# Where the first of two maxima pieces stands inside an output product

## The chip, the cores and the metric

The kernel runs on one core of one Trainium2 chip. The metric is the device time of one execution in microseconds; the median of three timed runs counts. One further execution was profiled, and all views of the profile come from it.

## The reference

Two multi-head attentions over 2048 positions, each with 32 heads of 18 columns, stand side by side in the output. A looks at 8 positions, two apart; B at all of them.

```python
def _A_ref(x, wqkv, wo):                    # B, S, D = 1, 2048, 576; H = 32; Dh = 18
    ...
    logits = jnp.einsum("bhsd,bhswd->bhsw", q, kg) * scale    # 8 neighbours, dilation 2
    ...
    o = jnp.einsum("bhsw,bhswd->bhsd", attn, vg)
    return (lambda x, *d: x.transpose(*d))(o, 0, 2, 1, 3).reshape(B, S, D) @ wo

def _B_ref(x, wqkv, wo):
    ...
    scores = jnp.einsum("bhqd,bhkd->bhqk", q, k) * scale
    p = _softmax(scores, axis=-1)
    o = jnp.einsum("bhqk,bhkd->bhqd", p, v)
    return (lambda x, *d: x.transpose(*d))(o, 0, 2, 1, 3).reshape(B, S, D) @ wo

a = _A_ref(A_x, A_wqkv, A_wo)
b = _B_ref(B_x, B_wqkv, B_wo)
return jnp.concatenate([a, b], axis=-1)
```

## The kernel before

The schedule is written out by hand: each engine runs its instructions in the order in which the Python code issues them, and a wait holds up all that stands behind it on that engine. After the projections (until about 500 us) come 512 steps of B. A step is one group of four heads, one block of 512 queries and one tile of 128 keys. In it TensorE computes four scores of 128 keys by 512 queries (`score`, line 229), one for each head; ScalarE takes their exponentials (line 235); and TensorE weighs the values with the exponentials of the step before (`weigh`, line 700, eight matmuls over all 128 rows of the array).

A score uses 56 rows of the array, and so the array is worked as two halves of 64 rows: heads 0 and 2 run on half 0, heads 1 and 3 on half 1.

The exponentials need the greatest score of each query beforehand. TensorE therefore also computes *maxima pieces*, 128 queries by 512 keys (`take`, line 159), and VectorE reduces each one to its maximum (`reduce`, line 166). A step normally holds three pieces. Each stands behind a score and runs on the other half (`maximum(1 - r)`).

Everything on TensorE ends in one of PSUM's eight banks. One (`po`) belongs to the weighing. Four form the ring "scores", three the ring "else"; `bank(kind)` gives the next of a ring, and the first matmul into it waits until the bank's last content has been read. Pieces use the ring "else", so that each one waits for the reduction of the piece (or the reading of the sum) that had its bank.

A's attention itself is computed by GpSimd beside all this, in eight runs of 256 positions, with a few small operations on VectorE and ScalarE (lines 850, 859, 866). Its output product (`sums_of_a`) is done in 32 parts, 128 positions by 288 columns, for which 27 matmuls of 288 columns are needed; B's output products (`sum_of`) have the same shape with 30. Both call `beside`, which deals the matmuls out to the two halves: 14 on half 0 and 13 on half 1 for A, 15 and 15 for B. Each half has a sum of its own, in a bank of "scores" and one of "else". `beside` issues them by turns, half 0, half 1, half 0 and so on (line 1001). ScalarE (line 918) and VectorE (line 919) add A's two sums; for B VectorE does both (lines 1020 and 1021).

A product stands inside a step, ahead of head 2 or head 3:

```python
if inside and h == (3 if 3 in places else 2):
    inside.pop(0)()
es.append(score(g, b, kt, h, h in places, ...))
```

As long as there are maxima to compute, `beside` puts two further pieces inside the product, one into each half's list. These are the "first" and the "second" piece. After the product a bank of "else" is passed over (`rings["else"].append(...)`), because it still holds a sum; the step's remaining piece, "the next piece" below, then takes the bank of the first one. Where the product stands ahead of head 2, head 2's score (half 0), the next piece (half 1) and head 3's score (half 1) come behind it; where it stands ahead of head 3, head 3's score (half 1) and the next piece (half 0).

Of the kernel before, what the change touches and what calls it, by code (L numbers as in the profile page):

```python
# [59 lines left out]
def two_attentions(ctx: ExitStack, tc, xa, wa, woa, xb, wb, wob, out):  # L60
# [19 lines left out]
    def bank(kind=None):  # L80
        r = rings[kind or ring]
        r.append(r.pop(0))
        return p_bank.tile([128, 512], F32, name=f"bank{r[-1]}")
# [124 lines left out]
    def maximum(r):  # L208

        n, i = divmod(given[r], PIECES)  # L210
        given[r] += 1
        if n not in blocks:
            blocks[n] = block(*divmod(n, NB))
        take, reduce = blocks[n]
        piece = (r, i // 2 // NB, i // 2 % NB, i % 2)
        ps = take(*piece)
        return lambda: reduce(ps, *piece)
# [121 lines left out]
    with (tc.tile_pool(name="x", bufs=1, side="right") as xp,  # L339
# [104 lines left out]
        if True:  # L444
# [238 lines left out]
            turns = len(work_list) - NT + 4  # L683
# [122 lines left out]
    def local(j):  # L806
# [103 lines left out]
        def sums_of_a(h):  # L910
            his, los = zip(*wo["a"])
            w = his[:4], los[:4], his[4], los[4]
            cols = slice(288 * h, 288 * h + 288)
            if h == 0:
                st["y"] = ys["a", j, st["n"]] = work.tile([128, D], F32, name="y", bufs=4)
            one, two = beside("scores", *(halves(r, 0, w, st["x"], cols, slice(0, 128), True) for r in range(2)))
            y = st["y"][:, cols]
            nc.scalar.activation(y, two, AF.Copy)
            behind_scores.append(lambda: nc.vector.tensor_add(y, one, y))
# [67 lines left out]
    def beside(kind, *both):  # L987

        sums_ = [bank(k)[:, :288] for k in (kind, None)]
        turns = [[(sums_[r], *ab, i == 0, i == len(t) - 1) for i, ab in enumerate(t)] for r, t in enumerate(both)]  # L990
        pair = kind and sum(given) + 2 <= NG * NB * PIECES * 2
        if pair:

            for r in range(2):
                turns[r].insert(4 + 6 * r, None)
        for i in range(max(map(len, turns))):
            for r in range(2):
                if i < len(turns[r]):
                    if turns[r][i]:
                        ps, a, b, start, stop = turns[r][i]  # L1000
                        nc.tensor.matmul(ps, a, b, start=start, stop=stop)  # L1001
                    else:
                        maximum(r)()
        if pair:

            rings["else"].append(rings["else"].pop(0))
        return sums_

    def sum_of(y, t, h, chunks, kind=None):

        pos, cols = slice(128 * t, 128 * t + 128), slice(288 * h, 288 * h + 288)
        both = []
        for r in range(2):
            both.append([])
            for c, (hi, lo) in enumerate(chunks):
                at = slice(64 * r, min(64 * r + 64, hi.shape[0]))
                whi, wlo = wo["b"][c]
                both[r] += [(a[at, pos], w[at, cols]) for a, w in ((hi, whi), (hi, wlo), (lo, whi))]
        one, two = beside(kind, *both)
        nc.vector.tensor_copy(y, one)  # L1020
        nc.vector.tensor_add(y, two, y)
# [149 lines left out]
```

## Time and profile before

| | |
|---|---|
| timed runs | 1653.38, 1653.39, 1655.6 us; median 1653.39 us |
| the profiled execution's own time | 1650.43 us |
| its span, first to last instruction | 1648.7 us, mean granted TensorE clock 0.999 |
| busy: TensorE, VectorE, ScalarE, GpSimd | 1639.2, 1400.6, 1223.6, 960.5 us |
| 2048 maxima reductions (L166) on VectorE | 1291.3 us, 684 ns each |
| 2048 exponentials (L235) on ScalarE | 1060.1 us, 611 ns each |

In the views, PE is TensorE's matmuls, PEld its weight loads, DVE VectorE, ACT ScalarE, POOL GpSimd, SP the engine that issues most transfers. L159 is line 159 of the kernel. A row of the timeline gives start, duration, engine, line, operation, output and inputs, shapes and a count, and in brackets how long the engine had been idle and what ended that. Matmuls are pipelined, so their durations overlap: the distance between two starts on one half is what a matmul costs there.

### The profile page before, as it was taken

What the parts mean: (1) busy time and instruction counts of PE and PEld (TensorE: products, weight loads), DVE (VectorE), ACT (ScalarE), POOL (GpSimd) and SP (SyncE); (2) the same over time, 40 slices, a digit from 0 to 9 for tenths busy, and PEclk for the clock granted to TensorE, in tenths of its full rate; (3) what the DMA queues carried; (4) which work ended last, traced back from release to release, by engine and by line L of the source; (5) the groups of instructions that cost most, each with busy time, mean ns of one, the idle gap of its engine ahead of it and who ended that gap; (6) DMA issues with size and microseconds to landing.
All of it is one profiled execution on the core that took longest, in us unless ns stands there. A gap on an engine that the chain in (4) does not pass through costs nothing.

```text
span 1648.7 us, 33732 instructions
## 1 busy us (share of the span) xinstructions
PE 1639.2 (99%) x12906; PEld 935.6 (57%) x12906; DVE 1400.6 (85%) x2386; ACT 1223.6 (74%) x2419; POOL 960.5 (58%) x800
## 2 busy tenths in 40 slices
PE   9999999999999999999999999999999999999999
PEld 7999788999433344344344344344344344344676
DVE  5199899999899989989889889889889989888533
ACT  6414432111899998998998998998998998998544
POOL 2306642210185995994994995994994997920000
PEclk9999999999999999999999999999999999999999
DMA  8937955522515346156238225617526132034201
GB/s 250 238 114 205 255 165 139 133 87 90 95 51 97 99 132 123 68 130 137 67 91 159 83 70 154 131 50 130 125 79 126 58 105 78 21 114 140 83 37 58
DMA packets 188353, 188.22 MB, mean 114 GB/s; under 512 B 118384, under 2 KB 132208, under 8 KB 186464
## 3 DMA queue, kind: packets, MB, share of 16 engines
q1 hardware_dynamic: 183328, 174.53, 40.2%
q0 software_dynamic: 4032, 10.63, 3.2%
q8 instruction: 101, 1.65, 0.4%
q10 hardware_dynamic: 832, 0.92, 0.2%
q14 instruction: 60, 0.49, 0.1%
HBM read 113.16 MB, written 88.12 MB: 122 GB/s over the span
## 4 chain that ended last, share of the span: by engine, by line
PE 96%; DMA 1%; DVE 1%; ACT 1%; issue 1%; POOL 0%; SPq 0%; POOLq 0%; ACTq 0%
PE po L700 30%; PE bank L229 26%; PE bank L322 15%; PE bank L159 13%; PE bank L1001 7%; PE bank L259 5%; DVE mx L166 1%; DMA dqk<-olo 0%; POOL xlo L370 0%; PE bank L976 0%; DMA dqk<-ohi 0%; DMA first<-xb 0%; ACT xhi L369 0%; SPq L363 0%; ACT olo L461 0%
## 5 line engine op out<-in xcount | busy, mean ns | idle before, releaser
L166 DVE TENSOR_REDUCE mx<-bank 128x1 f32<-128x512 f32 x2048 | 1291.3, 684 | 146.0 <-PE bank L159 108.5
L235 ACT ACTIVATE e<-bank 128x512 f32<-128x512 f32 x2048 | 1060.1, 611 | 91.2 <-PE bank L229 54.5
L159 PE MATMUL bank<-ks,qs 54*128 54x512 f32 x2048 | 751.4, 423 | 1.5 <-DVE mx L166 0.5
L229 PEld LDWEIGHTS bank<-qs,ks 56*128 56x128 f32 x2048 | 328.7, 185 | 449.5 <-ACT e L235 424.6
L229 PE MATMUL bank<-qs,ks 56*128 56x512 f32 x2048 | 579.4, 425 | 0.0
L700 PE MATMUL po<-e,v 128*19 128x512 f32 x4096 | 539.6, 599 | 0.0
L159 PEld LDWEIGHTS bank<-ks,qs 54*128 54x128 f32 x2048 | 341.8, 185 | 19.8 <-DVE mx L166 11.9
L832 POOL TENSOR_TENSOR pr<-aq,akv 128x1024 f32<-128x1024 f32 x72 | 158.4, 2200 | 27.2 <-DMA akv<-dpart 24.6
L700 PEld LDWEIGHTS po<-e,v 128*19 128x19 f32 x4096 | 69.5, 97 | 180.0 <-issue 169.5
L875 POOL TENSOR_TENSOR pr<-lg,akv 128x1024 f32<-128x1024 f32 x72 | 158.2, 2197 | 0.6
L836 POOL TENSOR_TENSOR pr<-pr 128x1024 f32<-128x1024 f32 x64 | 152.5, 2383 | 5.0
L651 ACT ACTIVATE ohi<-bank 128x512 f32<-128x512 f32 (+1 forms) x56 | 30.5, 595 | 147.6 <-issue 109.6
L322 PE MATMUL bank<-xhi,ahi 64*128 64x512 f32 (+1 forms) x448 | 114.1, 387 | 0.0
L322 PE MATMUL bank<-xhi,alo 64*128 64x512 f32 (+1 forms) x448 | 111.4, 387 | 0.0
L322 PE MATMUL bank<-xlo,ahi 64*128 64x512 f32 (+1 forms) x448 | 109.3, 388 | 0.2
L876 POOL TENSOR_TENSOR pr<-pr 128x512 f32<-128x512 f32 x72 | 92.2, 1281 | 5.6
L370 POOL TENSOR_TENSOR alo<-raw,ahi 128x512 fp32r<-128x512 f32 (+1 forms) x14 | 17.6, 1254 | 120.5 <-ACT ahi L369 105.8
L463 POOL TENSOR_TENSOR olo<-olo,ohi 128x512 fp32r<-128x512 f32 x36 | 46.1, 1294 | 66.2 <-ACT ohi L462 64.2
L1001 PE MATMUL bank<-wohi,at 64*128 64x288 f32 x512 | 68.5, 301 | 0.0
L322 PEld LDWEIGHTS bank<-xhi,ahi 64*128 64x128 f32 (+1 forms) x448 | 64.8, 181 | 3.5
L322 PEld LDWEIGHTS bank<-xhi,alo 64*128 64x128 f32 (+1 forms) x448 | 62.5, 182 | 3.5
L736 POOL TENSOR_TENSOR o<-o,rec 128x512 f32<-128x512 f32 x29 | 37.3, 1287 | 45.6 <-ACT e L235 24.7
(196 smaller groups left out, 1769.7 us busy)
## 6 DMA issues: line engine op xcount, KB each, us to landing
do<-n SPq DMA_DIRECT2D x28, 512.0 KB
da<-ohi SPq DMA_DIRECT2D x52, 256.0 KB
dpart<-da SPq DMA_DIRECT2D x16, 702.0 KB
akv<-dpart SPq DMA_DIRECT2D x16, 702.0 KB
out<-y SPq DMA_DIRECT2D x32, 288.0 KB
qs<-dqk SPq DMA_DIRECT2D x30, 288.0 KB
ks<-dqk SPq DMA_DIRECT2D x30, 288.0 KB
at<-dao SPq DMA_DIRECT2D x64, 128.0 KB
```

What stands on the lines that cost most here:

```text
L159: nc.tensor.matmul(ps, qs[at, b, p, 128 * t : 128 * t + 128], ks[at, p, 512 * k : 512 * k + 512], start=True, stop=True)
L166: nc.vector.tensor_reduce(mx[:, r, p, t, k : k + 1], ps, axis=AX.X, op=ALU.max)
L229: nc.tensor.matmul(ps, ks[at, p, 128 * kt : 128 * kt + 128], qs[at, b, p], start=True, stop=True)
L235: nc.scalar.activation(e, ps, AF.Exp, scale=SCALE)
L259: nc.tensor.matmul(ps, a, b, start=c == i == 0, stop=c == 4 and i == 1)
L322: nc.tensor.matmul(ps, a, b, start=start, stop=stop)
L700: nc.tensor.matmul(po[32 * i : 32 * i + 19], vs[g][:, kt, 19 * i : 19 * i + 19], es[i], start=kt == 0, stop=kt == NT - 1)
L832: nc.gpsimd.tensor_mul(pr, ap(st["q"][:, 2 * c], (SUB, 2), (0, W), (1, SUB)), window(st["k"], c))
L836: nc.gpsimd.tensor_add(st["pr"], st["pr"], pr)
L875: nc.gpsimd.tensor_mul(at, ap(st["lg"], (0, 2), (SUB, W), (1, SUB)), window(st["v"], c))
L876: nc.gpsimd.tensor_add(at[:, :, :4], at[:, :, :4], at[:, :, 4:])
L1001: nc.tensor.matmul(ps, a, b, start=start, stop=stop)
```

## The change

In `beside`, each half's list of matmuls gets a placeholder for its piece. Half 0's (`r = 0`) stood at place 4 and now stands at place 6; half 1's (`r = 1`) stays at place 10.

```diff
         if pair:
 
             for r in range(2):
-                turns[r].insert(4 + 6 * r, None)
+                turns[r].insert(6 + 4 * r, None)
```

So the first piece is issued behind six pairs of product matmuls instead of four, and four places ahead of the second piece instead of six. This concerns the 34 products with pieces in them: all 32 of A and two of B. Nothing is added or removed.

## The prediction

> **What bounds the kernel now.** I read the page first: engine shares, granted clock, the chain that ended last.
>
> ```profile
> PE 1639.2 (99%) x12906; PEld 935.6 (57%) x12906; DVE 1400.6 (85%) x2386; ACT 1223.6 (74%) x2419; POOL 960.5 (58%) x800
> PEclk9999999999999999999999999999999999999999
> PE 96%; DMA 1%; DVE 1%; ACT 1%; issue 1%; POOL 0%; SPq 0%; POOLq 0%; ACTq 0%
> ```
>
> TensorE (PE) is on 96% of the chain, at full clock throughout. A microsecond saved or lost on it is one of the span, unless another engine is late there. But "busy" counts modelled ends and hides short waits inside the stream. So next: the waits of weight loads (PEld), and VectorE's groups between 600 and 1520 us, which count the products that the change touches.
>
> ```profile
> PEld bank L159 <- DVE mx L166: 11.9, 41, 0.5
> L919 DVE TENSOR_TENSOR y<-bank,y 128x288 f32<-128x288 f32 x32 | 14.3, 448 | 0.0
> ```
>
> 41 times the load for a maxima piece (L159) waited for a maximum reduction (L166) on VectorE to free its PSUM bank, 11.9 us in all. The 32 rows of L919 are the sliding attention's output products; with two of the full attention's, in the last scheduled steps, 34 products hold two pieces each. In the two programs' instruction order just these 34 first pieces move on TensorE; the order on the other queues stays. Then I read the timeline of each of the 34. Here is one, TensorE's rows first, then its load, VectorE and ScalarE (ACT). Columns: start us, us, engine, line, what, count, idle before.
>
> ```profile
> 610.24 0.43 PE L1001 MATMUL bank<-wohi,at 64*128 64x288 f32 x4
> 610.51 0.29 PE L1001 MATMUL bank<-wolo,at 64*128 64x288 f32 x2
> 610.64 0.29 PE L1001 MATMUL bank<-wohi,at 64*128 64x288 f32 x2
> 610.99 0.49 PE L159 MATMUL bank<-ks,qs 54*128 54x512 f32 x1
> 610.99 0.40 PE L1001 MATMUL bank<-wohi,at 64*128 64x288 f32 x1
> 611.23 0.29 PE L1001 MATMUL bank<-wolo,at 64*128 64x288 f32 x1
> 611.32 0.33 PE L1001 MATMUL bank<-wohi,at 64*128 64x288 f32 x2
> 611.89 0.39 PE L159 MATMUL bank<-ks,qs 54*128 54x512 f32 x1
> 612.52 0.40 PE L159 MATMUL bank<-ks,qs 54*128 54x512 f32 x1
> 612.63 0.51 PE L229 MATMUL bank<-qs,ks 56*128 56x512 f32 x2
> 613.08 1.05 PE L700 MATMUL po<-e,v 128*19 128x512 f32 x8
> 610.98 0.18 PEld L159 LDWEIGHTS bank<-ks,qs 54*128 54x128 f32 x1 [0.28 <-DVE mx L166]
> 610.24 0.69 DVE L166 TENSOR_REDUCE mx<-bank 128x1 f32<-128x512 f32 x1 [0.22 <-PE bank L159]
> 610.85 0.68 DVE L166 TENSOR_REDUCE mx<-bank 128x1 f32<-128x512 f32 x1
> 611.51 0.69 DVE L166 TENSOR_REDUCE mx<-bank 128x1 f32<-128x512 f32 x1
> 612.34 0.69 DVE L166 TENSOR_REDUCE mx<-bank 128x1 f32<-128x512 f32 x1
> 612.73 0.41 ACT L918 ACTIVATE y<-bank 128x288 f32<-128x288 f32 x1 [1.44 <-PE bank L1001]
> ```
>
> L1001 x2 is a pair, one matmul on each half of the array. Pairs follow every 0.13 us (610.51, 610.64), so the first piece was due on half 0 at 610.77. Its bank was held by the reduction of 610.24, which ends at 610.93; the load starts 0.05 later, at 610.98, and nothing covers it: the piece shows 0.49 us, not 0.39, so I let it stream from 611.09. That is 0.32 us after it was due. Half 1's next product, behind it in the queue, waits too.
>
> **Part by part.** Nothing is added or removed; the first piece goes behind two more pairs. The second stands where it was.
>
> *Early products.* In 17 of the 34 the product stands ahead of head 2. The load of 610.98 is their first; the sixteenth:
>
> ```profile
> 1486.80 0.18 PEld L159 LDWEIGHTS bank<-ks,qs 54*128 54x128 f32 x1 [0.28 <-DVE mx L166]
> ```
>
> (The 17th, at 1533.5, waits alike.) Two more pairs take 2 x 0.13 = 0.27 us, unrounded, of the 0.32: the piece is due at 611.04 and, its bank being free when it was, still streams at 611.09, but with two pairs behind it instead of ahead. Gain so far 0.27.
>
> Then two banks come due sooner than before. The second piece takes the bank of the reduction at 610.85, free at 611.53: load 611.58, stream 611.68. Half 1 reaches it after four products (4 x 0.13) from 611.09, at 611.62, where it began at 611.89. Waits 0.06; gain 0.21. Third, the piece after the product, also on half 1, takes the first piece's own bank. That reduction starts at 611.51, as before, and ends at 612.20: load 612.25, stream 612.35. Half 1 gets there after a piece and three products. A piece holds its half 0.24 us, as a pair of rows of another product shows, of which more below:
>
> ```profile
> 634.65 0.42 PE L1001 MATMUL bank<-wohi,at 64*128 64x288 f32 x3
> 634.78 0.40 PE L159 MATMUL bank<-ks,qs 54*128 54x512 f32 x1
> 635.02 0.32 PE L1001 MATMUL bank<-wohi,at 64*128 64x288 f32 x2
> ```
>
> So it is due at 611.68 + 0.24 + 3 x 0.13 = 612.32, waits some 0.03, and streams at 612.35 against 612.52. Gain 0.165, my value (0.16 to 0.17 with unrounded starts). Queued behind this new wait are head 3's score (L229) on half 1 and the eight weighings (L700) at 613.08, which need both halves; they come 0.165 earlier. ScalarE waits for those scores, had been idle 1.44 us, and stays ahead. VectorE does two reductions 0.61 apart (610.24, 610.85); the second piece's comes at about 612.13 instead of 612.34, which it can serve. 17 x 0.165 = 2.8 us.
>
> The bounds of this term: 0 if the two new waits take all, 0.27 if they take none.
>
> *Late products.* In the other 17 the product stands ahead of head 3, and half 0 ends last. A typical one, then the one that waits longest:
>
> ```profile
> 640.98 0.52 PE L1001 MATMUL bank<-wohi,at 64*128 64x288 f32 x2
> 641.12 0.47 PE L159 MATMUL bank<-ks,qs 54*128 54x512 f32 x1
> 642.77 0.39 PE L159 MATMUL bank<-ks,qs 54*128 54x512 f32 x1
> 643.08 0.62 PE L700 MATMUL po<-e,v 128*19 128x512 f32 x3
> 641.63 0.69 DVE L166 TENSOR_REDUCE mx<-bank 128x1 f32<-128x512 f32 x1
> 888.56 0.18 PEld L159 LDWEIGHTS bank<-ks,qs 54*128 54x128 f32 x1 [0.18 <-DVE mx L166]
> ```
>
> Here half 0 still had head 2's score to finish, so its fourth product came at 640.98. The piece was due at 641.11 and streams from 641.20 (0.47 is 0.08 over 0.39): it lost 0.08, half 1 more, but half 1 has time left. Two places later it streams unhindered at 641.38; its reduction moves from 641.63 to 641.81 and ends at 642.50, so the next piece could stream at 642.65; it is due at 642.77 - 0.08 = 642.69. Gain 0.08, margin 0.04. Twelve like this gain 0.06 to 0.08: 12 x 0.07 = 0.85 us. Two with a later release (this load and one at 1386) lose about 0.2, and the shift covers it: 0.4. Three (634.78 above is one) come late for another reason and find their bank free: the piece shows 0.40 and follows its pair by 0.13. They gain nothing and lose nothing; their margin for the next piece is some 0.01 to 0.04.
>
> *Sum:* 2.8 + 0.85 + 0.4 = 4.05, say 4.0 us. The profiled execution took 1650.43 (span 1648.7 and 1.7 around it): it would be 1646.4. The median of the three timed runs is 1653.39, 3.0 above it; I take the gain off that: **1649.4 us**.
>
> *What a realignment may cost.* Steps after the first product run earlier against DMAs and GpSimd (POOL). The trace has two accidents of that kind, a transfer that VectorE met before it landed and a small tensor operation that took 1.33 us beside a GpSimd one:
>
> ```profile
> 907.97 0.25 DVE L733 RECIPROCAL den<-den 128x16 f32<-128x16 f32 x1 [1.25 <-DMA den<-o]
> 1376.27 1.33 DVE L850 TENSOR_TENSOR am<-am 128x64 f32<-128x64 f32 x1
> ```
>
> Each costs about 1 us. One may go or one may come: 0 taken, from -2 to +2.
>
> **Rivals.** *More gain.* If matmuls of the two halves had to start in program order, each 512-wide piece would hold up both; half 1 would then reach the second piece at about 611.72 and the next at 612.49, both after their banks are free, and the early products would keep the whole 0.27: 17 x 0.267 + 1.25 = 5.8 us, 1647.6. Against it: after the first piece the program has two wohi products, half 1's and half 0's, before the first wolo, yet the rows show one wohi at 610.99, the wolo at 611.23, and the other wohi at 611.32. So the halves pass each other. By the Trainium skill, "TensorE: Matmul & The Clock Gate", section "The mechanism", matmuls start and end strictly in program order even on different row groups; these rows differ from it, and by that rule it would be this rival. 12%.
>
> *Part of the gain.* The next piece's wait costs 0.10 more than I reckon, as the load exposed at 610.98 did: early products gain 0.065, 17 x 0.065 + 1.25 = 2.3 us, 1651.1. An accident more does the same. For it: the margins of 0.03 to 0.06 are at the edge of what the rows resolve. With the low end of my forecast, 26% within 0.2%.
>
> *Slower.* The next piece is tied to the first piece's bank. If that first piece were not waiting for the reduction of 610.24 but for something that moves along with it, such as a restart of TensorE, it would come 0.27 + 0.10 later than now: its reduction at 611.88, the next piece's stream at 612.72 instead of 612.52; in a late product at 642.84 instead of 642.77. 17 x 0.20 + 17 x 0.07 = 4.6 us, 1658.0. It decides from a reduction 0.17 late in the early products. Against it: the load follows the reduction's end by 0.05 us in every early product, and where the bank was free there was no wait. 9%.
>
> **How the numbers follow.** The bound of 0.2%, 3.3 us, is about what a measurement of this kernel can tell from no change. Forecast as worked out, gain over 3.3: 53%. With the 12% of more gain, faster 65%; same 26%; slower 9%. The range takes in the greater gain with an accident gone (5.8 + 1 = 6.8 us, 1646.6) and, at the other end, the partial gain with two accidents more (1653.1) and 0.9 us for the scatter of the timed runs, which lie 2.2 us apart (1653.38 to 1655.6): 1654.0. Slower by 4.6 is left out.
>
> **What would show it.** Early products: the first piece's load waits about 0.03 instead of 0.28 behind six pairs; the piece after the product starts about 2.11 us after the product's first row instead of 2.28, its load just behind the first piece's reduction; the L700 some 2.67 us after the product instead of 2.84. The row L159 <- L166 falls from 11.9 by about 4. Late products: L700 0.07 nearer. I am wrong if the first piece still waits as long, if its reduction in the early products comes later than 1.3 us after the product's start, or if the piece after it gives the 0.27 back.

## The result, and the profile after

The changed kernel is faster: 1649.07 us in the median of six runs (1645.07 to 1650.25) against 1655.57 of six runs of the kernel before (1653.38 to 1658.43); ratio 0.9962, 95% interval 0.9948 to 0.9976, that is 4 to 9 us. The profiled execution took 1648.65 us.

The page of the changed kernel has the same shape: TensorE at 99%, the clock full, the same instructions; on the chain that ended last, DMAs have 4% instead of 1%. The span, the engines, and the rows of waits that differ, of weight loads and of VectorE (total us, how often, the longest):

```profile
span 1646.9 us, 33732 instructions
PE 1635.5 (99%) x12906; PEld 938.5 (57%) x12906; DVE 1395.2 (85%) x2386; ACT 1222.5 (74%) x2419; POOL 960.6 (58%) x800
```

```profile
PEld bank L159 <- DVE mx L166: 8.8, 22, 2.0
DVE den L733 <- DMA den<-o: 4.7, 2, 3.1
```

The loads of pieces wait 22 times, not 41, but one of these waits is 2.0 us long. It belongs to the second row, VectorE's wait for `den`, of which below. Without it the first row falls by 5.1 us (11.9 to 6.8); about 4 was forecast. The timeline of the same early product as in the prediction, TensorE first, then the loads of its three pieces and VectorE:

```profile
610.52 0.43 PE L1001 MATMUL bank<-wohi,at 64*128 64x288 f32 x4
611.31 0.45 PE L159 MATMUL bank<-ks,qs 54*128 54x512 f32 x1
611.90 0.45 PE L159 MATMUL bank<-ks,qs 54*128 54x512 f32 x1
612.59 0.46 PE L159 MATMUL bank<-ks,qs 54*128 54x512 f32 x1
613.21 1.05 PE L700 MATMUL po<-e,v 128*19 128x512 f32 x8
611.26 0.18 PEld L159 LDWEIGHTS bank<-ks,qs 54*128 54x128 f32 x1
611.86 0.18 PEld L159 LDWEIGHTS bank<-ks,qs 54*128 54x128 f32 x1
612.55 0.18 PEld L159 LDWEIGHTS bank<-ks,qs 54*128 54x128 f32 x1
610.52 0.69 DVE L166 TENSOR_REDUCE mx<-bank 128x1 f32<-128x512 f32 x1 [0.23 <-PE bank L159]
611.80 0.69 DVE L166 TENSOR_REDUCE mx<-bank 128x1 f32<-128x512 f32 x1
```

The product starts at 610.52. The first piece's bank is free at 611.21 (610.52 + 0.69) and its load comes at 611.26, 0.74 us after the product's start, as before (610.98 - 610.24); but now six pairs lie ahead of it, and no idle time is noted at the load. Its reduction starts at 611.80, 1.28 after the start (1.27 before) and ends at 612.49; the next piece, in the same bank, loads at 612.55. All three pieces show 0.45 or 0.46 instead of 0.39: each load is a little exposed, by what is left of the first wait and by the two new waits of the prediction. L700 comes 2.69 us after the product's start instead of 2.84: 0.15 gained, 0.165 forecast.

For all products I took the step that holds it, from its L700 to the next step's, and subtracted the kernel before's. The early products' median is 0.15 us less, the late ones' 0.08 less. Over 33 products it is 4.0 us; the 34th, at 1379 us, is left out here and in the table below, since its step also holds the accident of 1376 us.

### The profile page after: what moved, and what is told of

Read it like the earlier page. It is cut to its first block, busy times and chain, and to the rows that moved or that the text cites. A ratio compares the mean times of both kernels' runs of the same rounds, so it can differ in the third digit from the quotient of the medians.

```text
span 1646.9 us, 33732 instructions
## 1 busy us (share of the span) xinstructions
PE 1635.5 (99%) x12906; PEld 938.5 (57%) x12906; DVE 1395.2 (85%) x2386; ACT 1222.5 (74%) x2419; POOL 960.6 (58%) x800
## 3 DMA queue, kind: packets, MB, share of 16 engines
q8 instruction: 101, 1.65, 0.4%
## 4 chain that ended last, share of the span: by engine, by line
PE 93%; DMA 4%; ACT 1%; DVE 1%; POOL 0%; issue 0%; SPq 0%; ACTq 0%; POOLq 0%
PE po L700 30%; PE bank L229 25%; PE bank L322 14%; PE bank L159 13%; PE bank L1001 7%; PE bank L259 3%; DMA den<-o 1%; DMA dqk<-olo 1%; DMA dqk<-ohi 1%; DMA first<-wb 1%; DMA raw<-xa 1%; POOL xlo L370 0%; DMA raw<-xb 0%; DMA first<-xb 0%; PE bank L976 0%
## 5 line engine op out<-in xcount | busy, mean ns | idle before, releaser
L700 PE MATMUL po<-e,v 128*19 128x512 f32 x4096 | 539.6, 599 | 0.0
L700 PEld LDWEIGHTS po<-e,v 128*19 128x19 f32 x4096 | 69.5, 96 | 179.7 <-issue 169.3
L322 PEld LDWEIGHTS bank<-xlo,ahi 64*128 64x128 f32 (+1 forms) x448 | 62.0, 182 | 5.2 <-POOL xlo L370 1.6
L1001 PE MATMUL bank<-wohi,at 64*128 64x288 f32 x512 | 64.5, 297 | 0.0
```

What stands on the lines that cost most here:

```text
L700: nc.tensor.matmul(po[32 * i : 32 * i + 19], vs[g][:, kt, 19 * i : 19 * i + 19], es[i], start=kt == 0, stop=kt == NT - 1)
```

## The experiments

### The first piece at places 5, 6, 7 and 8

```diff
-                turns[r].insert(4 + 6 * r, None)
+                turns[r].insert(5 + 5 * r, None)   # also 6 + 4 * r, 7 + 3 * r, 8 + 2 * r
```

Three theories were at stake: that of the prediction (banks and reductions); the rival by which the halves cannot pass each other; and a realignment, by which the gain came only from DMAs, GpSimd and VectorE meeting at other moments.

> First piece at place 5, second at 10. Bank theory (the first piece waits for the reduction that frees its bank, and the next piece for the first one's): the load still waits in the early products, one pair more is ahead of it, so the early products end 0.13 us sooner than in the kernel before and the typical late ones 0.07: 3.4 us in all. Program-order theory (halves cannot pass each other): the same 3.4 us. Realignment theory (the gain of the change came from other moments at which DMAs and VectorE meet): no relation to the place, anything within 3 us either way.

> The changed kernel again, first piece at place 6, on the same chip as its neighbours. Bank theory: 4.0 us less than the kernel before; early products 0.163 sooner, typical late ones 0.07. Program-order theory: 5.8 us less, early products 0.267 sooner; the first measurement (0.9962, about 6 us) leaves room for both. Realignment theory: another ratio than the first time, with no change inside the products needed.

> First piece at place 7. Bank theory: its own bank is long free, so nothing more is gained ahead of it, while its reduction comes later and the next piece, in the same bank, waits: early products 0.07 us sooner than before (0.09 worse than at place 6), typical late ones 0.03 later than before; 0.7 us less than the kernel before, so 3.3 us slower than place 6. Program-order theory: the next piece has time, no loss against place 6, 5.8 us less than before. Realignment theory: no relation.

> First piece at place 8, two ahead of the second. Bank theory: the next piece waits for the later reduction; early products 0.06 us later than in the kernel before, typical late ones 0.16 later: 3.7 us slower than before, 7.7 slower than place 6. Program-order theory: about 4.3 us less than before. Realignment theory: no relation.

All four ran on one chip, beside the kernel before (1649.56 us, 35 runs). The ratios are not quite the quotients of the medians; at place 7 the interval holds 1:

| first piece at | ratio, 95% interval | median us | change of 33 products, us | forecast for 34 |
|---|---|---|---|---|
| 5 | 0.9977, 0.9967 to 0.9986 | 1645.59 | -3.4 | -3.4 |
| 6 | 0.9974, 0.9965 to 0.9984 | 1645.14 | -4.0 | -4.0 |
| 7 | 1.0001, 0.9992 to 1.001 | 1648.79 | -1.0 | -0.7 |
| 8 | 1.0021, 1.0012 to 1.003 | 1652.65 | +3.2 | +3.7 |

The program-order theory wanted -5.8 at 7 and -4.3 at 8 and falls. A realignment without relation to the place falls too. Here is why 8 is slower, in the timeline of its first early product, the one shown above: its start, the three pieces and L700, then the third piece's load and the reduction of the first piece.

```profile
610.75 0.43 PE L1001 MATMUL bank<-wohi,at 64*128 64x288 f32 x4
611.81 0.40 PE L159 MATMUL bank<-ks,qs 54*128 54x512 f32 x1
612.09 0.49 PE L159 MATMUL bank<-ks,qs 54*128 54x512 f32 x1
612.99 0.49 PE L159 MATMUL bank<-ks,qs 54*128 54x512 f32 x1
613.65 1.05 PE L700 MATMUL po<-e,v 128*19 128x512 f32 x8
612.99 0.18 PEld L159 LDWEIGHTS bank<-ks,qs 54*128 54x128 f32 x1
612.25 0.69 DVE L166 TENSOR_REDUCE mx<-bank 128x1 f32<-128x512 f32 x1 [0.21 <-PE bank L159]
```

Now the first piece waits for nothing (0.40 us, no exposed load). Its reduction starts at 612.25, 1.50 us after the product's start instead of 1.28, and ends at 612.94; the next piece's load follows at 612.99. The two places that the first piece went back are paid by the next piece: L700 comes 2.90 us after the start. The prediction said that the sign turns when that reduction comes 0.17 later. At place 7 it is 1.36 after the start, and L700 at 2.76:

```profile
611.31 0.44 PE L1001 MATMUL bank<-wohi,at 64*128 64x288 f32 x4
612.67 0.69 DVE L166 TENSOR_REDUCE mx<-bank 128x1 f32<-128x512 f32 x1
613.42 0.50 PE L159 MATMUL bank<-ks,qs 54*128 54x512 f32 x1
614.07 1.05 PE L700 MATMUL po<-e,v 128*19 128x512 f32 x8
```

So against place 4's reduction at 1.27 and L700 at 2.84, 0.09 late still gains 0.08 and 0.23 late loses 0.06; between the two lies the 0.17.

### The tensor operation at 1376 us

The changed kernel's two steps around 1376 us are 1.27 us shorter, over and above the 33 products (the second step holds the 34th); places 5 and 6 show 1.28 and 1.23, place 7 nothing, and at 8 only one of the two is shorter, by 0.27. VectorE and GpSimd there, in the kernel before:

```profile
1375.96 1.64 DVE L850 TENSOR_TENSOR am<-am 128x128 f32<-128x128 f32 x2
1376.06 1.45 POOL L105 TENSOR_TENSOR ks<-y,qs 126x576 fp32r<-126x576 f32 x1
```

and in the changed one:

```profile
1376.11 0.88 DVE L850 TENSOR_TENSOR am<-am 128x128 f32<-128x128 f32 x2
1376.16 0.75 POOL L104 CAST qs<-y 126x576 fp32r<-126x576 f32 x1
1376.99 1.43 POOL L105 TENSOR_TENSOR ks<-y,qs 126x576 fp32r<-126x576 f32 x1
```

In the kernel before, GpSimd's subtraction L105 is under way when VectorE's second `am` comes (1376.27, 1.33 us, in the prediction): that ends at 1377.60, just behind GpSimd's, at 1377.51. In the changed kernel both `am` are through when L105 starts, at 1376.99; beside the cast L104 they take 0.88 us together. To see whether the place of the piece matters for this at all, only GpSimd's split was moved, in the kernel before (one profiled execution):

```diff
-        later(3, lambda: split_on(nc.gpsimd, hi[:n], lo[:n], raw[:n]))
+        later(4 if k == "b" else 3, lambda: split_on(nc.gpsimd, hi[:n], lo[:n], raw[:n]))
```

> The kernel before, only GpSimd's split of the late output weights (L104, L105) one step later. If VectorE's operation at 1376 us is held up by GpSimd's L105 beside it, its two am<-am rows take 0.88 us together instead of 1.64, and the two steps at 1374 and 1377 us together 1.27 us less, as in the changed kernel, with the first piece still at place 4. If the hold-up came from the late piece, it stays.

```profile
1371.35 0.77 DVE L850 TENSOR_TENSOR am<-lg 128x256 f32<-128x256 f32 x1
1373.85 0.53 DVE L850 TENSOR_TENSOR am<-am 128x128 f32<-128x128 f32 x2
1376.43 1.43 POOL L105 TENSOR_TENSOR ks<-y,qs 126x576 fp32r<-126x576 f32 x1
```

The pair takes 0.53 us, less than the 0.88 expected, with no GpSimd operation beside it, and the second step is 0.98 us shorter, with the piece still at place 4. The other 0.3 us that the changed kernel gains stays away: `am<-lg`, one step earlier, still takes 0.77 us. There VectorE meets GpSimd's cast L737, which this edit leaves where it is. In the kernel before:

```profile
1373.35 0.61 POOL L737 CAST n<-o 128x512 fp32r<-128x512 f32 x1
1373.45 0.79 DVE L850 TENSOR_TENSOR am<-lg 128x256 f32<-128x256 f32 x1
```

and in the changed one:

```profile
1373.98 0.41 DVE L850 TENSOR_TENSOR am<-lg 128x256 f32<-128x256 f32 x1
1374.14 0.72 POOL L737 CAST n<-o 128x512 fp32r<-128x512 f32 x1
```

In the kernel before, VectorE comes second and takes 0.79 us; in the changed one it comes first and takes 0.41, and GpSimd's cast takes 0.72 instead of 0.61. So the hold-up is one of the two engines' meeting, and the change removes it only by moving VectorE's work against GpSimd's.

### VectorE's wait for den

The other accident of the prediction is larger in the changed kernel's profile than it was before:

```profile
908.76 0.25 DVE L733 RECIPROCAL den<-den 128x16 f32<-128x16 f32 x1 [3.11 <-DMA den<-o]
1055.02 0.25 DVE L733 RECIPROCAL den<-den 128x16 f32<-128x16 f32 x1 [1.63 <-DMA den<-o]
```

4.7 us, 3.4 more than the 1.3 before; the two steps are 3.3 us longer. That is why this profile's span is only 1.8 us shorter: 4.0 from the products and 1.3 at 1376 us, less those 3.3, and its steps began 0.3 later. The other profiles of kernels with this reciprocal show 0.8 to 1.6. In the next two the reciprocal is issued three steps later:

```diff
-                      (7, lambda: nc.vector.reciprocal(den, den)),
-                      (8, lambda: load(drec[g, b].rearrange("i (p n) -> (i p) n", n=16), den)),
+                      (10, lambda: nc.vector.reciprocal(den, den)),
+                      (10, lambda: load(drec[g, b].rearrange("i (p n) -> (i p) n", n=16), den)),
```

> The kernel before with the reciprocal of the sums (L733) and the transfer behind it three and two steps later (10 in place of 7 and 8), so that VectorE does not come to it before its input has landed. If these waits are a cost that changes from run to run and adds to both kernels: VectorE's wait for den is gone, and the time falls by about the wait that the profiles show (1.3 us in the kernel before), with less scatter. If they cost nothing: no change.

> The changed kernel with the same edit to the reciprocal. Bank theory: against the kernel before with that edit it gains what the products gain, 4.0 us, and 1.3 us more if the tensor operation of 1.33 us beside GpSimd at 1376 us stays out of it as in the changed kernel's profile. If the change's whole effect lay in the den waits (realignment theory), the two kernels with the edit would take the same time.

The wait is gone from the profiles of both. The kernel before with this edit took 1648.73 us (ratio 0.9993, 0.9984 to 1.0002), which does not show that it is faster; the changed one took 1645.17 (0.9968, 0.9957 to 0.9979). They differ by 3.6 us. Against the kernel before with the same edit, the 33 products of the changed one are 3.8 us shorter and the two steps at 1376 us 1.2, so 5.0 was to be expected. The intervals allow it but do not show it. The two profiles do, once they are read from the first weighing (L700) on; that of the kernel before comes first here, that of the changed one second:

```profile
422.23 1.05 PE L700 MATMUL po<-e,v 128*19 128x512 f32 x8
426.09 1.05 PE L700 MATMUL po<-e,v 128*19 128x512 f32 x8
```

From there to the end of the span they take 1224.0 and 1219.0 us, 5.0 apart. But the first weighing came 3.9 us later in the second profile, ahead of everything that the edits touch. Over all profiles here it lies between 421.0 and 426.1 us, with no order by kernel: as much scatter as the effect that is looked for.

What the edit does settle: with no den wait in either kernel the gain is still there (the two intervals do not meet), which a pure realignment denied. Less scatter is not shown: the 12 runs of the kernel before with the edit lie within 3.4 us, and 24 without it within 7.9, but the 12 at place 6, with the earlier reciprocal, lie within 3.6.

### The 14th matmul on the other half

In late products half 0 ends last. Where the input's high part lies decides which half has 14 matmuls:

```diff
-                load(last.bitcast(F32)[64 * i : 64 * i + 64].rearrange("p (s n) -> p s n", s=2),
+                load(last.bitcast(F32)[64 * (i ^ n) : 64 * (i ^ n) + 64].rearrange("p (s n) -> p s n", s=2),
...
-            one, two = beside("scores", *(halves(r, 0, w, st["x"], cols, slice(0, 128), True) for r in range(2)))
+            one, two = beside("scores", *(halves(r, st["n"], w, st["x"], cols, slice(0, 128), True) for r in range(2)), place=6 - st["n"])
...
-                turns[r].insert(6 + 4 * r, None)
+                turns[r].insert(place + (10 - place) * r, None)
```

> The changed kernel, with half 1 in place of half 0 given the 14th matmul in the late sliding products (the extra half chunk of the inputs is loaded to the other partitions), and their first piece at place 5. Bank theory: half 0 ends the typical late products, and is relieved by one matmul: 0.13 us sooner than in the kernel before instead of 0.07, in 11 products; the two that waited longest give back 0.06 each; in all 0.6 us less than the changed kernel, 4.6 less than the kernel before. If the two halves had to go on in program order: no gain against the changed kernel.

1644.65 us, ratio 0.9968 (0.9958 to 0.9978). In the profile the late products' median is 0.125 less than in the kernel before, where the changed kernel has 0.08; the two long ones gave back 0.07 each. The 33 products are 4.3 us less, 0.3 better than the changed kernel rather than 0.6. The mechanism holds, product by product; the timed runs cannot tell so small a step from the changed kernel.

### The two together

> The swap of halves in the late products and the later reciprocal together, on the changed kernel. If the terms add: products 4.3 us less than in the kernel before, as the profile of the swap alone shows, 1.2 us less at 1374 to 1377 us, and about 1 us less for VectorE's wait for den: 6.5 us in all, a ratio near 0.996, below the changed kernel's 0.9974. If the later reciprocal only moves VectorE's work into the way of other reductions, it stays at the swap's 0.9968.

1643.08 us, ratio 0.9931 (0.9917 to 0.9944): more than the sum, because the kernel before took 1654.83 us beside it (9 runs), not 1650. So it was measured again, with the kernel before under the profiler once more and with the later reciprocal alone:

> The kernel before once more, for a second profile. If VectorE's wait for den is what differs between executions and chips, it is another than 1.3 us here, while the 34 products take what they took (within 0.3 us in all) and the am<-am rows near 1376 us again take 1.64 us together.

> The kernel before with the later reciprocal again, on the chip of the next kernel. If the den waits explain that the kernel before was some 5 us slower beside the last kernel than in the jobs before it, this kernel takes 1648 to 1649 us again on any chip, and the gap to the kernel before is what changes.

> The last kernel again, swap and later reciprocal together. Sum of the terms: 0.996 of the kernel before, and 5 to 6 us less than the kernel before with the later reciprocal alone (products 4.3, and 1.1 to 1.3 at 1374 to 1377 us). The 0.9931 measured once would come again only where the kernel before itself takes about 1655 us.

This time the kernel before took 1650.58 us (15 runs) and the combination 1644.00, ratio 0.9958 (0.9946 to 0.9971), the sum of the terms; its 33 products are again 4.3 us less. The later reciprocal alone took 1648.95 (0.9988, 0.9979 to 0.9997), and the combination about 5 us less. From the first weighing on, the two profiles with the later reciprocal alone take 1224.0 and 1224.2 us, the two of the kernel before 1225.4 and 1225.2: the den wait of 1.1 to 1.3 us is a cost that the edit takes away. The second profile of the kernel before repeats the first: the products within 0.03 us in sum, `am<-am` 1.65 us, a den wait of 1.1. The combination has the lowest medians here, on both occasions, but the swap alone was measured on another chip, and the second ratio's interval holds the swap's 0.9968; that the combination is faster than the swap is not shown. Why the kernel before takes about 1655 us in some places (here, and in the first measurement of the change) and 1650 in others I could not show: none of its profiles shows an execution of that length. The granted clock goes along with part of it: 8 of those 9 runs have 0.998 or 0.999, and of the 35 runs of the first experiment the 24 at 1.0 took 1649.1 us in the mean, the 9 at 0.999 1650.8 and the 2 at 0.998 1652.6. It is not all, for the ninth run had 1.0 and took 1655.65.

## Why the prediction was right, and where not

- *The wait and its owner.* Right: a load that waited follows the reduction's end by 0.05 us (the median of each kernel), whatever the place. In the early products the first piece's load still comes at 0.05 at places 4, 5 and 6; at places 7 and 8 its bank is free before it is due, and the load comes 0.10 to 0.12 and 0.24 to 0.26 us behind the release.
- *Early products, 0.165 us each.* Measured 0.15 in the median. One of the 17, at 740 us, gained nothing. There VectorE does a small reduction (L173) between the second bank's reduction and the first piece's. In the kernel before, it delays a reduction that nobody is waiting for; in the changed one the next piece waits for it:

```profile
741.32 0.22 DVE L173 TENSOR_REDUCE m<-mx 128x16 f32<-128x64 f32 x1
741.46 0.68 DVE L166 TENSOR_REDUCE mx<-bank 128x1 f32<-128x512 f32 x1
742.19 0.18 PEld L159 LDWEIGHTS bank<-ks,qs 54*128 54x128 f32 x1
742.85 1.05 PE L700 MATMUL po<-e,v 128*19 128x512 f32 x8
```

  The reduction of 741.46 ends at 742.14 and the load follows at 742.19. I had costed one typical product and multiplied; the margin of 0.03 us could not carry a 0.22 us operation. The 17th is odd the other way: B's product, at 1533.5 us, has 15 matmuls on each half, so that half 1 reaches the next piece later; in the changed kernel its load comes 0.24 us behind its bank's release and waits for nothing. The product gains 0.24, and 0.23 at places 7 and 8 as well.
- *Late products.* 0.06 to 0.08 forecast, 0.08 in the median; the two with the later release gained 0.20 each, as said. Of the three that come late for another reason two gained about 0.03 for nothing, and the third is the one at 1379 us.
- *The sum.* 4.05 forecast; 4.0 over 33 products. The timed gain is 6 us (4 to 9) the first time and 4.3 (2.6 to 5.8) the second.
- *The time.* 1649.4 us forecast, 1649.07 measured. That the two are so close is luck: over its six runs the kernel before took 1655.57, 2.2 more than the 1653.39 that the forecast started from, and the medians lie 6.5 apart, 2.5 more than the forecast gain. The profiled execution, 1646.4 by the forecast, took 1648.65: its den waits put on more (3.3) than the hold-up at 1376 us took off (1.3).
- *Realignment, taken as 0.* This is the term that was off. One of its two accidents is no chance: the hold-up at 1376 us is in both profiles of the kernel before, in both with the later reciprocal alone and at places 7 and 8, and in none of those whose products are 3.4 us or more shorter. In the profiles it adds about 1.3 us to the gain; the timed runs are too coarse to show it. The other, the den wait, varies from 0.8 to 4.7 us between profiles with no order by the place.
- *The rivals.* More gain by program order fell at places 7 and 8. Part of the gain (2.3 us) falls with the 4.0 us of the products. Slower had a wrong premise, that the first piece waits for something which moves with it; but the price it put on a late reduction is what place 8 pays, and its turning point lies between 7 and 8.

## What to carry to other kernels

Where an engine that is "99% busy" runs through a small ring of banks, follow the ring: who freed this bank, and who is next in it. Moving a matmul behind other work gains until its own bank is free; each place beyond that is charged to the next user of the bank. And cost the odd members of a series singly: a small operation that lies in slack today is on the path once the slack is used up.

## What the runs showed of the hardware

Matmuls on the two halves of the array start out of program order: the rows of 610.99, 611.23 and 611.32 in the prediction show it. By a strict order the kernels with places 7 and 8 would have been 5.8 and 4.3 us faster than the kernel before; they measured 1.0001 and 1.0021 of its time.

VectorE's operation with two inputs in SBUF was held until GpSimd's subtraction ended: 1.33 us for 128x64 (1376.27 to 1377.60, GpSimd 1376.06 to 1377.51), and the pair 1.64 us beside L105, 0.88 beside a cast, 0.53 with nothing beside it. Beside the cast, too, the pair ends just behind GpSimd's operation: at 1376.99, the cast at 1376.91. So what VectorE pays is what is left of GpSimd's operation when it comes. The Trainium skill says, in "SBUF — State Buffer", section "Who interferes with whom", that a VectorE instruction with two SBUF inputs contends with a GpSimd instruction that reads SBUF, and calls the contention for the shared ports an exclusive lock. These rows agree. What I had not expected is that one such meeting adds 1.3 us to the 4.0 of a change that moves no instruction of either engine.
